# One list of pieces in place of four, in a chunked attention and cosine feed-forward kernel on one core

## The chip, the core and the metric

The kernel runs on one core of a Trainium2 chip. The metric is the time of one execution in microseconds of that core. TensorE (PE) does the matrix products, ScalarE (ACT), VectorE (DVE) and GpSimd (POOL) the elementwise work, and SyncE (SP) issues every DMA of the loops from one queue.

## The reference, cut to what matters

```python
def _attn_ref(q, k, v):                 # 8 batches, 8 heads, 576 tokens, head size 64, chunks of 64
    scores = scale * np.matmul(q_c, k_c.transpose(0, 1, 2, 4, 3))
    scores = scores - np.max(scores, axis=-1, keepdims=True)
    attn = np.exp(scores)
    attn = attn / (np.sum(attn, axis=-1, keepdims=True) + 1e-09)
    out = np.matmul(attn, v_c)
...
def _moe_ref(x, w_in, w_out):           # x 4608 x 512, w_in 512 x 2048, w_out 2048 x 512
    h = x @ w_in
    g = h * np.cos(h)
    return (g @ w_out).astype(np.float32)
```

Attention is done within chunks of 64 tokens. Its output, 4,608 rows of 512, goes through a feed-forward layer with the activation h·cos(h). All is float32.

## The kernel before, in words

The rows are cut into nine tiles of 512 tokens. The feed-forward layer runs over 16 blocks of 128 hidden units (`fc`, 0 to 15). Every float32 operand of a product is split into a high and a low part, and a product is the sum of three matrix products (high·high, high·low, low·high).

**Stage 1** takes tiles 1 and 0 in 32 steps `s` (L1207). Each step makes one block of h (`hidden`, 12 matmuls into one of two `h` banks), then h·cos(h) by a chain of six operations (`activated`, L690: ACT, DVE, ACT, DVE, a copy to the high part, a subtraction for the low part), and, three steps later (`LAG`), four out pieces (`project`, three matmuls each, one per block of 128 rows). The attention of tiles 0, 1 and 2 is woven in. The products of steps 29 to 31 are left for stage 2.

**Stage 2 and later** handle tiles in pairs with a scheme of seven products (A11, S3, S2, A12, A22, S1, S4) in place of eight. It wants the weights `w_in` as sums of blocks ("combos"). They are computed in stage 1 on DVE, ACT and POOL (L1285 to L1296, and `combined`, L1794), stored to DRAM (`keep_blocks`, `keep_sums`, 256 KB each, 56 of them) and streamed back, two combos at a time, into rooms of the `w_in` tiles (`load_two`, L854). A streamed load has seven rooms at first and four (`KEPT_ROOMS`) afterwards: when the second product of a room has been issued, the room is loaded again. In the first round (28 loads) a load is two DMAs of 256 KB, later one of 512 KB. Tile 2 is done by `two_pairs` (four rounds of seven products and 16 out pieces), tiles 3 and 4, 5 and 6, 7 and 8 by eight `wide_pair` and one `second_tile` each (units u = 1, 2, 3).

**The order** is written out by hand in tables. Each step is a *piece* (`piece`, L1007): an engine, an estimated length, a function that emits its instructions, the pieces that it comes after, and a `lag` after its end. The numbers of a piece (length, lag, predecessors) served the planner that made the tables; the kernel at hand reads only the tables: `in_order` (L258) sorts the pieces by their rank and emits them, and a second table names the pieces that go to their other engine. Every instruction is kept in the order of its engine's list (`tc.keep_in_program_order`), and waits on data are put in as needed. There are four lists: stage 1; tile 2 with unit 1; unit 2; unit 3 (742, 1,010, 596 and 463 pieces). `emit` (L1321) and `close` (L1354) put a list out, empty it and clear all links, so that a piece of one list names no piece of an earlier one:

```python
    def close(wanted, *when):
        emit(wanted, *when)
        stream[0] = last_high[0] = None
        for d in (spent, low_of, acc_free, readers, ...): d.clear()
```

Two sorts of transfers are no pieces before: the streamed loads of `product` (L938) come wherever the PE piece stands that frees the room, and the stores of finished output rows (`finish`, L761) are left free to be placed.

Of the kernel before, what the change touches and what calls it, by code (L numbers as in the profile page):

```python
# [90 lines left out]
RANK_FIRST = (  # L91
# [33 lines left out]
)  # L125

ELSEWHERE_FIRST = (
# [7 lines left out]
RANK_SECOND = (  # L135
# [53 lines left out]
)  # L189


RANK_NEXT = (
# [1756 lines left out]
```

## Time and profile before

| | us |
|---|---|
| median of 3 runs | 797.67 (797.0 to 797.83) |
| the profiled execution | 796.2 |
| its span, first to last instruction | 794.4 |
| PE busy in the span | 773.2 |
| mean granted PE clock | 0.993 |

The profile is of one execution. Its time is 1.8 us over its span (launch and end), and 1.5 us under the median. "PE busy" counts the time in which at least one matmul is in flight.

### The profile page before, as it was taken

The page shows a single profiled execution, that of the slowest core. Times are in us where ns is not written, and L with a number is a line of the kernel's source. Part 1 is how long each engine was busy: PE and PEld are TensorE (multiplying, and loading weights), DVE is VectorE, ACT ScalarE, POOL GpSimd, SP SyncE. Part 2 cuts the span into 40 slices and gives each one's busy share as a digit, 9 for nine tenths or more (in the row PEclk, how much of TensorE's full clock was granted, in tenths as well). Part 3 has the DMA queues.
Part 4 walks back from the last instruction along what each step waited for, and adds up shares of the span by engine and source line. Part 5 has one row for each costly group of instructions (what it writes and reads, how often), then busy time and mean ns, then how long its engine had stood idle before and what let it go on. Part 6 is the DMA issues. An engine that isn't in the chain of part 4 may idle for free.

```text
span 794.4 us, 15040 instructions
## 1 busy us (share of the span) xinstructions
PE 773.2 (97%) x5818; PEld 676.2 (85%) x5818; DVE 589.0 (74%) x1031; ACT 431.3 (54%) x782; POOL 177.5 (22%) x158
## 2 busy tenths in 40 slices
PE   7999999997799999999999999999999999999997
PEld 6888888885798898888888888888888888888886
DVE  6998878997588868877788788776796756465632
ACT  5998876463485555554564256445533555445220
POOL 1352038735234352010110131100110200001010
PEclk9999999999899999999999999999999999999999
DMA  9994305248899764774555656666365164555441
GB/s 337 406 418 179 107 1 173 100 167 290 288 330 293 245 227 134 239 238 146 186 158 199 211 176 214 221 215 224 122 194 178 41 205 153 173 171 160 159 127 59
DMA packets 75928, 156.19 MB, mean 197 GB/s; under 512 B 7632, under 2 KB 22224, under 8 KB 75856
## 3 DMA queue, kind: packets, MB, share of 16 engines
q1 hardware_dynamic: 75856, 155.22, 57.2%
q8 instruction: 46, 0.75, 0.4%
q14 instruction: 26, 0.21, 0.1%
HBM read 117.44 MB, written 37.75 MB: 195 GB/s over the span
## 4 chain that ended last, share of the span: by engine, by line
PE 87%; DMA 9%; SPq 1%; ACT 1%; DVE 1%; issue 0%; DVEq 0%; ACTq 0%
PE acc L299 45%; PE h L299 33%; PE a L299 10%; DMA w_in<-combo 3%; DMA combo<-w_in 2%; DMA vt<-in_v_dram 2%; SPq L296 1%; DMA x<-partial 1%; DMA qt<-in_qT_dram 1%; DVE pts L614 0%; ACT w L380 0%; PE a L588 0%; ACT x L659 0%; ACT half L382 0%; ACT L699 0%
## 5 line engine op out<-in xcount | busy, mean ns | idle before, releaser
L299 PE MATMUL acc<-w_out,g_hi 128*128 128x512 f32 x1124 | 336.1, 381 | 5.8 <-ACT g_hi L316 5.8
L299 PEld LDWEIGHTS acc<-w_out,g_hi 128*128 128x128 f32 x1124 | 209.5, 189 | 35.3 <-ACT g_hi L316 6.2
L299 PE MATMUL h<-x,w_in 128*128 128x512 f32 (+1 forms) x960 | 228.5, 367 | 4.4 <-DMA w_in<-combo 4.1
L299 PE MATMUL acc<-w_out,g_lo 128*128 128x512 f32 x562 | 212.9, 379 | 0.0
L299 PEld LDWEIGHTS h<-x,w_in 128*128 128x128 f32 x960 | 172.5, 192 | 26.9 <-issue 4.3
L320 POOL TENSOR_TENSOR g_lo<-g,g_hi 128x512 fp32r<-128x512 f32 x35 | 47.7, 1364 | 356.4 <-DVE g_hi L314 192.4
L299 PEld LDWEIGHTS acc<-w_out,g_lo 128*128 128x128 f32 x562 | 106.3, 189 | 15.4 <-POOL g_lo L320 0.2
L299 PE MATMUL h<-w_in,w_in 128*128 128x512 f32 (+1 forms) x384 | 97.9, 353 | 0.6 <-DMA w_in<-combo 0.6
L299 PEld LDWEIGHTS h<-w_in,w_in 128*128 128x128 f32 x384 | 66.2, 190 | 8.8 <-DMA w_in<-combo 0.8
L316 ACT CAST g_hi<-g 128x512 fp32r<-128x512 f32 x61 | 37.8, 619 | 53.5 <-PE acc L299 30.9
L320 DVE TENSOR_TENSOR g_lo<-g,g_hi 128x512 fp32r<-128x512 f32 x73 | 54.6, 752 | 16.2 <-ACT g_hi L316 14.5
L951 DVE SCALAR_TENSOR_TENSOR g<-g,h 128x512 f32<-128x512 int32 x28 | 19.2, 686 | 52.4 <-ACT g L948 52.1
L955 ACT ACTIVATE g<-g 128x512 f32<-128x512 f32 x56 | 35.2, 629 | 20.6 <-DVE g L951 20.4
L299 PE MATMUL a<-w_in,w_in 128*128 128x512 f32 (+1 forms) x192 | 41.2, 353 | 0.4 <-DMA w_in<-combo 0.4
L299 PE MATMUL a<-x,w_in 128*128 128x512 f32 (+1 forms) x192 | 41.2, 353 | 0.0
L942 ACT COPY h<-h 128x512 f32<-128x512 f32 x28 | 16.0, 570 | 40.3 <-PE h L299 34.1
L299 PEld LDWEIGHTS a<-w_in,w_in 128*128 128x128 f32 x192 | 33.2, 190 | 4.8 <-issue 0.8
L955 ACT ACTIVATE w_in<-w_in 128x512 f32<-128x512 f32 x48 | 29.9, 628 | 12.4 <-DVE w_in L951 12.1
L299 PEld LDWEIGHTS a<-x,w_in 128*128 128x128 f32 x192 | 33.1, 190 | 4.0
L942 ACT COPY a<-h 128x512 f32<-128x512 f32 x28 | 16.1, 574 | 36.5 <-PE h L299 36.3
L697 ACT ACTIVATE g<-h 128x512 int32<-128x512 f32 x32 | 19.0, 597 | 26.4 <-PE h L299 24.7
L698 DVE SCALAR_TENSOR_TENSOR g<-g,h 128x512 f32<-128x512 int32 x32 | 21.7, 681 | 9.9 <-ACT g L697 9.7
(219 smaller groups left out, 1161.6 us busy)
## 6 DMA issues: line engine op xcount, KB each, us to landing
w_in<-combo SPq DMA_DIRECT2D x84, 512.0 KB, 3.7
combo<-w_in SPq DMA_DIRECT2D x56, 256.0 KB, 3.3
w_in<-combo SPq DMA_DIRECT2D x56, 256.0 KB, 5.1
gathered<-w_in SPq DMA_DIRECT2D x48, 256.0 KB, 3.5
qt<-in_qT_dram SPq DMA_DIRECT2D x36, 256.0 KB, 5.2
kt<-in_kT_dram SPq DMA_DIRECT2D x36, 256.0 KB, 5.3
w_in<-in_w_in_dram SPq DMA_DIRECT2D x16, 512.0 KB, 9.6
w_out<-in_w_out_dram SPq DMA_DIRECT2D x16, 512.0 KB, 9.6
```

The source lines that it names most:

```text
L296: kept(nc.sync.dma_start(out=out, in_=in_))
L299: kept(nc.tensor.matmul(*args, **kw))
L316: kept(nc.scalar.copy(out=out, in_=in_))
L320: kept(eng.tensor_tensor(out, a, b, op=op))
L697: lambda: kept(nc.scalar.activation(n, h, AF.Identity, bias=0.25, scale=0.5 / math.pi)),
L698: lambda: kept(nc.vector.scalar_tensor_tensor(g, n, -2.0 * math.pi, h, op0=turns, op1=over)),
L942: kept(nc.scalar.copy(out=out, in_=in_))
L951: kept(nc.vector.scalar_tensor_tensor(g, g.bitcast(I32), -2.0 * math.pi, h, op0=ALU.mult, op1=ALU.add))
L955: kept(nc.scalar.activation(g, g, AF.Sin, bias=0.5 * math.pi))
```

## The change

All 2,949 pieces stand in one list with one table of ranks, put out once at the end. The links that `close` cut are made: the first pieces of stage 2 now name the pieces of stage 1 that they need. Each streamed load and each store of output rows is a piece on SP with a rank of its own, and the stores are kept in order. The `lag` of nearly all SP pieces, 2.5 to 5.0 before, is 2.0. No arithmetic, tile or transfer is added or taken away.

```diff
-def in_order(work, wanted, rank, elsewhere):
+def in_order(work, rank, elsewhere):
...
-        nc.sync.dma_start(out=to, in_=os)
+        made_rows[t, sub, half, whole] = (to, os)
+    def store_rows(t, sub, half=None, whole=True):
+        to, os = made_rows.pop((t, sub, half, whole))
+        kept(nc.sync.dma_start(out=to, in_=os))
...
-        if n % 2 and fc in KEPT_ROOMS:
-            load_two(fc)
...
-        kept_sums[k] = piece(SP, 2.6, lambda k=k: keep_sums(k), lows[-1], lag=3.5)
-        for fc in (2 * k, 2 * k + 1):
-            if STREAM <= fc < STREAM + ROOMS:
-                piece(SP, 1.3, lambda fc=fc: load_two(fc, fc - STREAM), kept_sums[k], kept_sums[1], kept_sums[0])
+        kept_sums[k] = piece(SP, 2.6, lambda k=k: keep_sums(k), lows[-1], lag=2.0)
+    stream_room = list(range(STREAM, STREAM + ROOMS))
+    def stream_in(i, *after):
+        fc, q = stream_room[i], i // 7
+        first = i < len(combos)
+        stored_pairs = [d[k] for d in (kept_blocks, kept_sums) for k in (2 * q, 2 * q + 1)] if first else []
+        stream_here[i] = piece(SP, 1.3, lambda: load_two(fc, i), *after, *stored_pairs, lag=2.0)
...
-    emit([(i, -4.0) for i in parts_x + [kept_sums[k] for k in range(3)] + [summed]], RANK_FIRST, ELSEWHERE_FIRST)
+    low_of.update({(0, NFC - LAG + i): given[STAGE - LAG + i] for i in range(LAG)})
+    readers.update({
+        "h1": [held[STAGE - 2]], "h0": [held[STAGE - 1]], "a0": [banks_free["a", 0]], "a1": [banks_free["a", 1]],
+        "h2": [kept_sums[1], kept_blocks[1]], "more": [hids[-1]], "differences": [hids[-1]],
+    })
...
     def product_piece(n, length, run, *after):
-        p = pe(length, run, *after, stored_sums.get(n))
+        p = pe(length, run, *after, stream_here[n // 2])
         if n % 2:
-            room_done[n // 2] = p
+            i = n // 2
+            room_done[i] = p
+            if stream_room[i] in KEPT_ROOMS and len(stream_room) < UNITS * len(combos):
+                stream_room.append(stream_room[i])
+                stream_in(len(stream_room) - 1, p)
...
-            close([], RANK_LAST, ELSEWHERE_LAST)
             break
...
+    for i, by in in_order(work, RANK, ELSEWHERE):
+        work[i][2](*([by] if work[i][8] else []))
```

The tables are long rows of ranks, and a piece's number is its place in the order of the calls of `piece`. Read off in that way, the orders around the seam between stage 1 and tile 2 are these (out s/b is the out piece of step s and row block b, fc 13 to 15 of tile 0 are the products of steps 29 to 31, st0 to st6 are streamed loads):

```
PE before: hidden 30, 4 outs of step 28, hidden 31 | out fc14, scores 3a, scores 3b, 9 outs of fc13-15,
           A11, S3, S2, A12, A22, S1, 2 outs, S4, scores 4a
PE after:  hidden 30, hidden 31, 3 outs of step 28, 1 of step 27, scores 3a, 1 out of step 28, out fc13, scores 3b,
           out fc13, A11 (half), 3 outs of fc13-15, A11 (half), 2 outs, S3, S2, A12, A22, S1, 3 outs, S4, 2 outs, scores 4a
SP before: ... sums 2, sums 3, sums 5, q and k of tile 3, blocks 7, st6, st1, st0, partial rows, blocks 6, sums 4,
           st4, st3, st5, st2 | q and k of tile 4, ...
SP after:  ... blocks 4, blocks 6, sums 1, blocks 3, blocks 5, sums 3, blocks 7, tile 1's rows, q and k of tile 3,
           sums 4, sums 2, sums 5, st5, st4, st1, st0, partial rows, st2, st6, v of tile 3, st3, q and k of tile 4, st7, ...
```

## Rows read from the trace of the kernel before

**Rows 1.** Busy time by stretch, whole span: us, busy by engine, PEclk, DMA share, GB/s.

```profile
0.00:20.00 20.00, 14.61 (x292) 12.30 (x292) 12.24 (x25) 11.84 (x34) 3.22 (x8) 1.00 0.92 337
20.00:190.00 170.00, 169.77 (x1260) 146.88 (x1252) 153.46 (x263) 126.89 (x210) 75.72 (x73) 1.00 0.52 196
190.00:200.00 10.00, 4.25 (x19) 2.79 (x22) 4.29 (x7) 3.07 (x6) 1.27 (x1) 0.82 1.05 381
...
280.00:780.00 500.00, 500.00 (x3288) 437.06 (x3287) 352.55 (x607) 239.77 (x400) 68.35 (x50) 1.00 0.54 177
780.00:795.00 15.00, 9.64 (x51) 8.27 (x49) 3.39 (x6) 1.26 (x3) 0.00 (x0) 0.96 0.19 71
```

**Rows 2.** Waits of PE, whole span: us in total, times, longest us.

```profile
PE acc L299 <- ACT g_hi L316: 5.8, 1, 5.8
PE h L299 <- DMA w_in<-combo: 4.7, 2, 4.1
```

**Rows 3.** Timeline of PE, 188 to 265 us: start, us, instruction, [idle before <- releaser].

```profile
189.81 2.75 PE L299 MATMUL h<-x,w_in 128*128 128x512 f32 x12
198.31 1.22 PE L299 MATMUL acc<-w_out,g_hi 128*128 128x512 f32 x2 [5.75 <-ACT g_hi L316]
...
216.27 4.54 PE L299 MATMUL h<-x,w_in 128*128 128x256 f32 x24 [4.12 <-DMA w_in<-combo]
...
226.06 0.27 PE L299 MATMUL h<-kt,qt 64*64 64x64 f32 x1
...
227.15 0.70 PE L299 MATMUL acc<-w_out,w_in 128*128 128x512 f32 x2
...
243.77 0.94 PE L299 MATMUL h<-w_in,w_in 128*128 128x256 f32 x6 [0.57 <-DMA w_in<-combo]
...
263.73 0.91 PE L299 MATMUL a<-w_in,w_in 128*128 128x256 f32 x6 [0.38 <-DMA w_in<-combo]
```

**Rows 4.** Busy time by stretch around the seam, columns as in rows 1.

```profile
196.30:203.20 6.90, 4.89 (x127) 4.10 (x131) 2.50 (x5) 1.07 (x3) 0.00 (x0) 0.51 1.04 370
205.00:214.00 9.00, 7.15 (x45) 6.42 (x43) 8.92 (x17) 7.05 (x35) 2.76 (x3) 1.00 0.59 168
216.80:220.20 3.40, 3.40 (x19) 3.40 (x18) 0.29 (x1) 1.11 (x2) 0.00 (x0) 0.50 1.07 390
```

**Rows 5.** Timeline of ACT after hidden 31.

```profile
192.66 1.09 ACT L697 ACTIVATE g<-h 128x512 int32<-128x512 f32 x2 [2.45 <-PE h L299]
```

**Rows 6.** The chain that ended last, 160 to 272 us: start, us, what.

```profile
162.04 1.09 PE a L299 x64
...
176.92 2.59 PE acc L299 x12
179.51 2.59 PE h L299 x12
...
269.88 1.34 PE h L299 x12
```

**Rows 7.** Timeline of the SP queue: DMA issues around the seam.

```profile
163.34 1.29 SPq L761 DMA_DIRECT2D out_dram<-pts  x2
...
189.93 4.16 SPq L296 DMA_DIRECT2D w_in<-combo  x6
...
...
207.59 3.66 SPq L296 DMA_DIRECT2D w_in<-combo  x8
```

**Rows 8.** Waits of the SP queue, 170 to 265 us.

```profile
SPq L296 <- DMA combo<-w_in: 7.8, 4, 5.9
```

**Rows 9.** DMA, 185 to 275 us: traffic, then issues, KB each, median us to landing.

```profile
DMA packets 17345, 27.44 MB, mean 305 GB/s; under 512 B 1680, under 2 KB 6327, under 8 KB 17335
...
w_in<-combo SPq DMA_DIRECT2D x50, 256.0 KB, 5.2
```

**Rows 10.** DMA issues, 300 to 780 us.

```profile
w_in<-combo SPq DMA_DIRECT2D x80, 512.0 KB, 3.7
```

**Rows 11.** Waits of the SP queue, whole span.

```profile
SPq L761 <- ACT half L316: 23.4, 4, 13.9
```

More of the change, by code (lines that the diff above doesn't have):

```diff
@@ L848, in w_in_room, with load_two @@
         return wts.tile([P, 2 * TOK + PAD], dtype, name=f"w_in{fc}")
-    asked = [ROOMS]
     UNITS = 1 + (NT - FAST) // 2
-    def load_two(fc, i=None):
-        if i is None:
-            i = asked[0]
-            asked[0] += 1
+    def load_two(fc, i):
         if i < UNITS * len(combos):
@@ L929, in product @@
     def product(n, out, x_hi, x_lo, begin=False):
-        w, fc = streamed[n // 2]
+        w, _ = streamed[n // 2]
         w = w[:, n % 2]
@@ L1051, in attention_then_cos_ffn @@
     turn_of = sorted(due, key=lambda b: (due[b], b))
+    u = None
     for i, (name, fc) in enumerate(turn_of):
@@ L1055, in attention_then_cos_ffn @@
         back = turn_of[i - 2] if i > 1 else None
-        u = piece(ACT, 0.52, rest_of(key, 0), split.get(back), at=here[name, fc])
+        u = piece(ACT, 0.52, rest_of(key, 0), split.get(back), u, at=here[name, fc])
         l = piece(ACT, 0.52, rest_of(key, 1), joined.get(back), at=here[name, fc])
@@ L1124, in values_next @@
                         load_v(t, j)
-                more_values = piece(SP, 1.3, values_next, now, lag=3.0)
+                more_values = piece(SP, 1.3, values_next, now, lag=2.0)
             for i in (0, 2):
@@ L1181, in values_next @@
                         load_v(t, hp)
-                third_here.append(piece(SP, 1.3, values_next, w, lag=3.0))
+                third_here.append(piece(SP, 1.3, values_next, w, lag=2.0))
             for i in range(2):
@@ L1189, in queries_next @@
                 load_qk(t + 1, hp)
-        piece(SP, 5.2, queries_next, w)
+        queries_at.append(piece(SP, 5.2, queries_next, w, lag=2.0))
         return w
@@ L1205, in attention_then_cos_ffn @@
     third = None
+    begun = None
     third_here = []
+    queries_at = []
     for s in range(STAGE):
@@ L1215, in attention_then_cos_ffn @@
                 stream = piece(
-                    PE, 0.648, go, stream if cc else None, split["in", fc], bank_at, *x_done[t][2 * cc : 2 * cc + 2],
+                    PE, 0.648, go, stream if cc else begun, split["in", fc], bank_at, *x_done[t][2 * cc : 2 * cc + 2],
                     *(all_turned if s < 2 else ()), pairs=3, main=True,
                 )
+                begun = begun if cc else stream
             before.append(stream)
@@ L1229, in prefetch_third @@
                     load_qk(2, hp)
-            third_here.append(piece(SP, 5.2, prefetch_third, ahead[HP - 1], stream, lag=3.0))
+            third_here.append(piece(SP, 5.2, prefetch_third, ahead[HP - 1], stream, lag=2.0))
         if s >= LAG:
@@ L1248, in attention_then_cos_ffn @@
                     out_of[run_of[u] + 1, sub] = done
-                    stored.append(piece(SP, 0.65, lambda: None, done, lag=2.5))
+                    stored.append(piece(SP, 0.65, lambda tu=tu, sub=sub, fu=fu: store_rows(tu, sub, None, fu == NFC - 1), done, lag=2.0))
                     if u < GROUP:
-                        partial_out.append(done)
+                        partial_out.append(stored[-1])
                 if u < GROUP:
@@ L1256, in values_third @@
                             load_v(2, hp)
-                    third_here.append(piece(SP, 1.3, values_third, *partial_out, lag=3.0))
+                    third_here.append(piece(SP, 1.3, values_third, *partial_out, lag=2.0))
         key = ("g", s)
@@ L1273, in attention_then_cos_ffn @@
             third = attend_third(hid)
-    piece(SP, 2.6, resume, hid)
+    resumed = piece(SP, 2.6, resume, hid, lag=2.0)
     kept_blocks = {}
@@ L1282, in attention_then_cos_ffn @@
         kept_blocks[k] = piece(
-            SP, 2.0, lambda k=k: keep_blocks(k), split["in", 2 * k], split["in", 2 * k + 1], hids[GROUP + 6 + k], lag=3.5
+            SP, 2.0, lambda k=k: keep_blocks(k), split["in", 2 * k], split["in", 2 * k + 1], hids[GROUP + 6 + k], lag=2.0
         )
@@ L1296, in attention_then_cos_ffn @@
         lows.append(piece(DVE, 1.7, lambda by, k=k: low_parts(k, by), a, port=True, other=(POOL, 3.6, False)))
-        kept_sums[k] = piece(SP, 2.6, lambda k=k: keep_sums(k), lows[-1], lag=3.5)
-        for fc in (2 * k, 2 * k + 1):
-            if STREAM <= fc < STREAM + ROOMS:
-                piece(SP, 1.3, lambda fc=fc: load_two(fc, fc - STREAM), kept_sums[k], kept_sums[1], kept_sums[0])
+        kept_sums[k] = piece(SP, 2.6, lambda k=k: keep_sums(k), lows[-1], lag=2.0)
+    stream_room = list(range(STREAM, STREAM + ROOMS))
+    stream_here = {}
+    def stream_in(i, *after):
[3 more added lines that the diff above has]
+        stream_here[i] = piece(SP, 1.3, lambda: load_two(fc, i), *after, *stored_pairs, lag=2.0)
+    for i, fc in enumerate(stream_room):
+        stream_in(i, kept_sums[fc // 2], kept_blocks[fc // 2])
     def of_x(i, *args):
@@ L1319, in attention_then_cos_ffn @@
         parts_x.append(piece(DVE, 0.69, of_x(2, j), a, port=True))
-    def emit(wanted, *when):
-        for i, by in in_order(work, wanted, *when):
-            work[i][2](*([by] if work[i][8] else []))
-        work.clear()
-    emit([(i, -4.0) for i in parts_x + [kept_sums[k] for k in range(3)] + [summed]], RANK_FIRST, ELSEWHERE_FIRST)
     queue = deque((0, fc, sub) for fc in range(NFC - LAG, NFC) for sub in range(NSUB))
@@ L1348, in attention_then_cos_ffn @@
     g_pool = deque([(0, NFC - 3), (0, NFC - 2), (0, NFC - 1)])
-    g_extra = deque([None])
-    g_free = deque([None, None])
     queries_read = deque()
     keys_read = [()] * HP
-    def close(wanted, *when):
-        emit(wanted, *when)
-        stream[0] = last_high[0] = None
-        for d in (
-            spent, low_of, acc_free, readers, room_done, stored_sums, kept_g, queries_here, values_here, weighed,
-            taken, turned_all, x_lows, asked_out,
-        ):
-            d.clear()
-        for q, nothing in ((g_free, None), (queries_read, ()), (keys_read, ())):
-            for i in range(len(q)):
-                q[i] = nothing
+    low_of.update({(0, NFC - LAG + i): given[STAGE - LAG + i] for i in range(LAG)})
[3 more added lines that the diff above has]
+    })
+    g_free = deque(given[STAGE - 2 + i] for i in range(2))
+    spent["room"] = [kept_sums[2], kept_blocks[2]]
+    g_extra = deque(["room"])
+    for g in range(2):
+        queries_here[FAST + 1, g] = queries_at[0]
+    weighed[FAST] = parts_x
+    for i, j in enumerate((A11, S3, S2, A12, A22, S1, S4)):
+        x_lows[FAST, j] = [parts_x[i]]
     def pe(length, run, *after):
@@ L1380, in out_piece @@
             PE, 0.648 if half is None else 0.336, lambda: out_part(t, fc, sub, half), low_of.get(made_of(t, fc, sub)),
-            acc_free.get(sub), main=True,
+            acc_free.get(sub), *(by_run[2, sub] if t == 0 else ()), main=True,
         )
@@ L1388, in out_piece @@
             if len(made[half]) == 2:
-                piece(ACT, 0.4, lambda: finish(t, sub, acc[sub], True, ACT, half), *made[None], *made[half])
+                p = piece(ACT, 0.4, lambda: finish(t, sub, acc[sub], True, ACT, half), *made[None], *made[half])
+                piece(SP, 0.35, lambda: store_rows(t, sub, half), p, lag=2.0)
         elif not to_come[t, sub, half]:
             if t == 0:
-                acc_free[sub] = piece(DVE, 0.7, lambda: finish(t, sub, acc[sub], True, None), *made[None])
+                acc_free[sub] = piece(DVE, 0.7, lambda: finish(t, sub, acc[sub], True, None), *made[None], resumed)
             else:
                 acc_free[sub] = piece(
-                    ACT, 0.62, lambda by: finish(t, sub, acc[sub], True, by), *made[None], other=(DVE, 0.69, False)
+                    ACT, 0.62, lambda by: finish(t, sub, acc[sub], True, by), *made[None],
+                    *(rows_stored[t - 1] if t > FAST else [kept_sums[7]]), other=(DVE, 0.69, False),
                 )
+            rows_stored.setdefault(t, []).append(piece(SP, 0.65, lambda: store_rows(t, sub), acc_free[sub], lag=2.0))
     to_come = {}
+    rows_stored = {}
     def outs(n=None):
@@ L1453, in go @@
                     product(
-                        14 * q + 2 * j + i, v[out][:, i * HALF : (i + 1) * HALF], halves_x[j][:, 0], halves_x[j][:, 1],
+                        14 * q + 2 * j + i, v[out][:, i * HALF : (i + 1) * HALF], x_halves[FAST][j][:, 0], x_halves[FAST][j][:, 1],
                         bool(begin) and not i,
                     )
-                done[j] = product_piece(14 * q + 2 * j + i, 0.672, go, *(() if i else deps))
+                x = x_lows[FAST, j] if q == 0 else ()
+                done[j] = product_piece(14 * q + 2 * j + i, 0.672, go, *(() if i else (*deps, *x)))
             return done[j]
@@ L1590, in keep @@
                 kept(nc.sync.dma_start(out=gathered[fc], in_=v[g]))
-            kept_g[fc] = piece(SP, 0.65, keep, m, lag=4.0)
+            kept_g[fc] = piece(SP, 0.65, keep, m, lag=2.0)
         readers["kept"] = [kept_g[2 * k], kept_g[2 * k + 1]]
@@ L1616, in second_tile @@
                     free = [g_free.popleft(), g_free.popleft()]
-                here = piece(SP, 1.3, begin, kept_g[fc], kept_g[fc + 1], *free, lag=4.2)
+                here = piece(SP, 1.3, begin, kept_g[fc], kept_g[fc + 1], *free, lag=2.0)
             lows[fc] = parts_of_g(t, fc, lambda fc=fc: v[fc], here)
@@ L1640, in queries_for @@
             free = [i for hp in (2 * g, 2 * g + 1) for i in (*queries_read.popleft(), *keys_read[hp])]
-            queries_here[t, g] = piece(SP, 2.6, go, *free, lag=5.0)
+            queries_here[t, g] = piece(SP, 2.6, go, *free, lag=2.0)
     def values_for(t, *after):
@@ L1647, in go @@
                     load_v(t, hp)
-            free = () if t == FAST + 1 else x_taken()
+            free = x_taken()
             if g:
                 free = [room_done[T_LOAD]] if t == FAST + 1 else [*free, *queries_read.popleft(), *queries_read.popleft()]
-            values_here[t, g] = piece(SP, 1.3, go, *after, *free, lag=4.5)
+            values_here[t, g] = piece(SP, 1.3, go, *after, *free, lag=2.0)
     def scores_now(t):
@@ L1809, in parts @@
             return lows
-        l6 = parts(6)
-        k6 = piece(SP, 2.6, lambda: keep_sums(6), *l6, lag=4.0)
+        l6 = parts(6, summed, kept_blocks[6])
+        k6 = kept_sums[6] = piece(SP, 2.6, lambda: keep_sums(6), *l6, lag=2.0)
         w7 = piece(DVE, 1.38, lambda by: whole_again(7, by), *l6, port=True, other=(POOL, 2.5, False))
         s7 = piece(DVE, 1.7, lambda by: sums_of_w(7, by), w7, port=True, other=(POOL, 3.0, False))
-        k7 = piece(SP, 2.6, lambda: keep_sums(7), *parts(7, s7), k6, lag=4.0)
-        rooms = list(range(STREAM, STREAM + ROOMS))
-        for n in range(1, 7 * NPAIR, 2):
-            if rooms[n // 2] in KEPT_ROOMS:
-                last = 2 * (len(rooms) // 7) + 1
-                stored_sums[n] = k7 if last >= 7 else k6 if last >= 6 else None
-                rooms.append(rooms[n // 2])
+        k7 = kept_sums[7] = piece(SP, 2.6, lambda: keep_sums(7), *parts(7, s7, kept_blocks[7]), k6, lag=2.0)
         stored_sums["six"] = k6
@@ L1835, in attention_then_cos_ffn @@
             if n_pair == 0:
-                first_copies = list(acc_free.values())
+                first_copies = list(rows_stored[0])
             n_pair += 1
@@ L1889, in attention_then_cos_ffn @@
             outs()
-            close([], RANK_LAST, ELSEWHERE_LAST)
             break
-        ends = wide_x(t, lambda j, part: [used])
-        ends += [(low_of[t - 1, NFC - 2], 0.0), (low_of[t - 1, NFC - 1], 0.0)]
-        close(ends, *((RANK_SECOND, ELSEWHERE_SECOND) if u == 1 else (RANK_NEXT, ELSEWHERE_NEXT)))
+        wide_x(t, lambda j, part: [used])
+    for i, by in in_order(work, RANK, ELSEWHERE):
+        work[i][2](*([by] if work[i][8] else []))
 _OUTS = [((4608, 512), "float32")]
```

22 lines of the change are left out of this document (3 added, 19 removed), and 300 rows, old and new, of tables (ELSEWHERE, ELSEWHERE_FIRST, ELSEWHERE_SECOND, RANK).

## The prediction

> **What bounds the kernel now.** I read first the busy time by stretch [rows 1]. From 20 to 190 us PE is busy for 169.77 of 170 us and from 280 to 780 us for 500 of 500, at the full clock: there the time is matmul work, and the change adds and removes none. The first 20 us have 5.4 us without a matmul and the end has 5.4 us (15 less 9.64, some 0.6 of it past the span). What is left lies between 190 and 280 us, around the seam between the first and the second list. Then the waits of PE [rows 2] name two: 5.8 us for a high part of g, 4.1 us for a streamed load. The timeline [rows 3] puts them: hidden 31 begins at 189.81 and ends at 192.56; the next matmul is an out piece at 198.31, after 5.75 us; then 4.12 us before 216.27, and 0.57 and 0.38 us later. Sum 10.82 us.
>
> The stretches around them [rows 4] show a second cost. From 196.3 to 203.2 and from 216.8 to 220.2 us the granted clock is half, 1.2 GHz in place of 2.4, each time just after PE had stood still. PE was busy for 4.89 and 3.40 us in them; at half speed half of that is lost, 4.1 us. So the seam costs 10.8 + 4.1 = 14.9 us.
>
> **Why PE stands there.** The first wait: the last pieces of list one put g's first step of steps 30 and 31 together at 192.66 [rows 5], after hidden 31, and the second list, which knows nothing of g, begins with an out piece of step 30. So PE has nothing in hand for the length of a chain of six operations. The second wait is SP's: it issued three streamed loads at 189.93 and the next ones only at 207.59 [rows 7], having waited up to 5.9 us for a store of combos to land [rows 8]. In the meantime, 205 to 214 us, the DMA engines were 0.59 busy [rows 4], while they were full from 190 to 200 [rows 1] and at 217 [rows 4].
>
> **The change, part by part.** *Order at the seam.* After hidden 31 PE now gets four outs of steps 27 and 28, scores 3a, an out, an out of fc13, scores 3b, an out of fc13 and half of A11 before an out of fc14, and one more out before fc15. Durations: an out 0.65 (four in 2.59), a hidden 2.59, two products of six matmuls 1.34 [rows 6], one group of scores 1.09 (226.06 to 227.15) [rows 3]. That is 4 x 0.65 + 1.09 + 0.65 + 0.65 + 1.09 + 0.65 + 0.67 = 7.4 us before fc14, and 8.1 before fc15. The chain needed 5.75 us, and g of step 30 now starts ahead of hidden 31's end. The four outs used to run before hidden 31, so this adds no work; hidden 31 merely comes 3.2 us (five outs) sooner, near 186.6. The 5.75 us go. Cover: if those outs and scores were themselves late (scores need the two h banks, freed by the chains of steps 30 and 31), at worst the same 5.75 us come back. DVE, which carries the chains, was busy for only 4.29 of the 10 us after 190 [rows 1], so there is room.
>
> *Loads at the seam.* SP's order is new: combos 6 and 7 (blocks) and sums 4 go ahead of the partial rows, and st5, st4, st1, st0 are issued right behind sums 5. The data before them: tile 1's rows (1 MB, at 163.34 as now [rows 7], right after the weighted products of tile 2 at 162.04 [rows 6]), q and k of tile 3 (2 MB), sums 4, 2 and 5 (3 MB). At the 381 GB/s of the full queue [rows 1] 6 MB take 15.7 us, to 179, and landed near 182. The four loads (2 MB) take 5.5 us and land near 190. A11 is wanted at 186.6 + 2.6 + 6.7 = 195.9, so it has 6 us in hand. The partial rows wait for hidden 31 (189.2), then 1 MB, st2, st6, v of tile 3 and st3 (3 MB, 7.9 us) are in near 200 with 3 us for the landing; S2 and A12, their first users, come at 195.9 + 0.67 + 1.94 + 0.67 + 1.30 + 1.34 = 201.8 and after. The 4.12 us go too. Bounds: 0, if the sum above holds, to 4.12, the wait now; as the margins are 2 to 6 us I take 0.7, near the lower end.
>
> *Later loads of the first round.* Their room is freed by a product, and the PE work between that and the use, counted from the tables with the durations above, is the cover. Before, the shortest are 4.7 us (loads 12 and 26); after, 4.7 (load 18) and 5.3 (12, 19). A load of this stretch lands 5.2 us after its issue [rows 9], and the wait of 0.57 us at 243.77 [rows 3] is load 12, as 5.2 less 4.7 says. The wait of 0.38 us is load 18, which SP issued behind sums 7; now it stands ahead of them. So I take 0.5 us for load 18 and bound it by 0 and 3 (all three late, DMA fuller). The Trainium skill, DMA: Bandwidth & Descriptors, section "Anatomy of one DMA", gives a DMA (of GpSimd's path) a fixed 2.0 us plus its bytes at 436 GB/s, which is also the lag that the new pieces carry. By it 256 KB land in 2.6 us (an estimate from that page), load 18 is not late, and the sum would be 0.5 us lower; the row's 5.2 speaks against it here.
>
> *Links, ranks and stores elsewhere.* In the wide units a load lands in 3.7 us [rows 10] and the new tables leave at least 5.3 us of PE work behind its place. Inside the old lists PE waited for 0.23 us in 20 to 190 and for nothing in 280 to 780 [rows 1]; I take 0.2 us for the whole new list, bounds 0 to 3. The 33 stores of rows are issued as before, now at fixed places. The first 14 PE pieces and the loads ahead of the lists are in the same order: 0, bounds -0.5 to +0.5. At the end the last two copies go to two engines instead of one, the last store is issued as late: 0, bounds -0.3 to +0.3.
>
> *Clock.* With no wait over 1 us at the seam the 4.1 us come back; that hangs on the two waits above.
>
> **Sum.** 14.9 - 0.7 - 0.5 - 0.2 = 13.5 us. The profiled execution of 796.2 us (span 794.4, 1.8 around it) becomes 782.7; the median shown is 1.5 above it, so 797.67 becomes **784.2 us**.
>
> **Rivals.** *The DMA takes over as the bound.* For: from 190 on the queue is full, and 185 to 275 us moved 27.44 MB at 305 GB/s [rows 9]; PE cannot run 15 us ahead of data that arrive no sooner. Then the gain is what the queue itself wins: its idle share in 205 to 214, 0.41 x 9 = 3.7 us [rows 4], and the 1.75 MB (blocks 6, sums 4) stored ahead of the first loads, 4.6 us at 381 GB/s. Together 8.3: 789.4 us. Against: all of stage 1 up to 190 used the engines by half only [rows 1], and the new order fills that.
>
> *The wait is moved, not removed.* PE finds another operand late at the seam (scores behind the h banks, x behind DVE), and its clock falls again: one wait of 5.75 us and half of 4.1 stay, 7.8 less gain, 792 us. Should all of it return, there is no change. Against: more than 7 us of ready work stand in the table.
>
> *Slower: the fixed SP order holds loads back in the wide units.* SP has waited for up to 13.9 us with one store of rows for a copy [rows 11], while such stores were free to be placed; now rows, gathered g and streamed loads stand in one fixed order. (The Trainium skill, DMA: Bandwidth & Descriptors, same section, says that a DMA's semaphore wait happens on the issuing sequencer, before dispatch; by that rule what stands behind it in the queue waits as well, and the row agrees that SP stood.) If each of the 24 wide pairs got one load 0.8 us late, 19 us go: 803 us. It decides from 0.65 us a pair on (15.1 in all). Against: the shortest cover of 5.3 us is 1.6 above the landing time.
>
> **How the numbers follow.** Forecast 0.67 (782.8, with nothing late, to 787); DMA bound 0.16; moved wait 0.07 with a gain, 0.03 without; slower 0.07. Range 782.5 to 791: it holds the first two and their bounds. A measurement here can tell about 0.2%, 1.6 us, from no change. Faster 0.67 + 0.16 + 0.07 = 0.90, same 0.03, slower 0.07.
>
> **What would show it.** Right: PE's busy time is some 769 us (773.2 less 4.1), the granted clock stays full from 20 us to the end, no PE wait over 1 us after 20 us, the first A11 comes 12 to 14 us sooner, SP issues st0 before hidden 31 begins. Wrong: a PE wait on w_in<-combo of several us between 190 and 260 us (DMA bound), on g_hi or g (moved wait), or many waits of under 1 us after 280 (slower).

## The result, and the profile after

The changed kernel takes 784.36 us (median of 4 runs, 783.78 to 785.35); the kernel before, on the same chip, 797.51 us (4 runs, 797.0 to 797.83). The ratio is 0.9837, interval 0.982 to 0.9854. The profiled execution of the changed kernel took 784.27 us, its span 782.5.

Busy time by stretch of the changed kernel, columns as in [rows 1]:

```profile
0.00:20.00 20.00, 14.79 (x292) 13.00 (x292) 11.27 (x22) 10.90 (x32) 5.55 (x11) 0.91 0.91 336
20.00:190.00 170.00, 169.09 (x1262) 146.63 (x1252) 156.17 (x274) 127.38 (x211) 73.93 (x70) 1.00 0.59 217
190.00:200.00 10.00, 10.00 (x170) 8.53 (x169) 9.19 (x17) 7.31 (x26) 3.96 (x5) 1.00 0.96 339
200.00:210.00 10.00, 9.30 (x73) 8.84 (x72) 6.92 (x14) 7.44 (x25) 4.28 (x5) 1.00 1.05 387
210.00:220.00 10.00, 10.00 (x173) 8.64 (x172) 8.91 (x18) 7.61 (x16) 4.48 (x3) 1.00 0.79 288
...
240.00:280.00 40.00, 39.51 (x407) 36.58 (x398) 31.60 (x58) 23.29 (x42) 13.62 (x11) 1.00 0.73 241
...
sum 780.00, PE 769.79 PEld 673.64 DVE 577.54 ACT 435.54 POOL 186.33; mean PE 96.22 PEld 84.21 DVE 72.19 ACT 54.44 POOL 23.29
```

From 190 to 200 us PE had been busy for 4.25 us at a clock of 0.82 [rows 1]; now it is busy for all 10 at the full clock, and DVE for 9.19 in place of 4.29. The half-clock stretches of [rows 4] are gone. What is left at the seam is 0.70 us and 0.49 us. The waits of PE say for what:

```profile
PE acc L304 <- DMA kt<-in_kT_dram: 1.9, 1, 1.9
PE h L593 <- POOL e L325: 1.7, 3, 1.0
...
PE h L304 <- DMA w_in<-combo: 1.2, 2, 0.7
```

The wait for g_hi of [rows 2] is gone; the 4.7 us for w_in<-combo are 1.2. The two larger waits lie in the first 20 us. Timeline of PE (as [rows 3]) and of the SP queue (as [rows 7]) at the seam of the changed kernel:

```profile
184.45 5.34 PE L304 MATMUL h<-x,w_in 128*128 128x512 f32 x24
...
196.74 0.83 PE L304 MATMUL h<-x,w_in 128*128 128x256 f32 x6
...
204.86 1.62 PE L304 MATMUL h<-x,w_in 128*128 128x256 f32 x12 [0.70 <-DMA w_in<-combo]
```

```profile
187.22 3.67 SPq L301 DMA_DIRECT2D w_in<-combo  x8
190.99 3.07 SPq L301 DMA_DIRECT2D x<-partial  x4
194.80 3.19 SPq L301 DMA_DIRECT2D w_in<-combo  x4
198.10 1.23 SPq L301 DMA_DIRECT2D vt<-in_v_dram  x2
199.46 0.96 SPq L301 DMA_DIRECT2D w_in<-combo  x2
```

Hidden 30 and 31 are the 24 matmuls from 184.45, so 31 begins near 187.0 and ends at 189.6. A11, the first line with 128x256 tiles, begins at 196.74. Before, it began at 209.31, so it comes 12.6 us sooner; PE's timeline of the kernel before:

```profile
209.31 1.50 PE L299 MATMUL h<-x,w_in 128*128 128x256 f32 x12
```

SP issues four loads (two DMAs of 256 KB each) ahead of the partial rows, where it had issued three and then waited until 207.59 [rows 7].

To place the difference, one cut serves for all kernels of this study: the hidden that waits for g just behind 28 us in every trace. From its start to the end of the last matmul each has the same 5406 matmuls. The busy time of that stretch, first in the kernel before, then in the changed one:

```profile
28.62:789.64 761.02, 750.19 (x5406) 657.02 (x5406) 566.98 (x987) 411.09 (x735) 173.50 (x150) 0.99 0.56 191
```

```profile
29.19:777.10 747.91, 746.72 (x5406) 653.60 (x5406) 556.54 (x972) 415.22 (x747) 177.48 (x154) 1.00 0.57 194
```

This middle part became 13.11 us shorter: PE's idle time in it fell from 10.83 to 1.19 us, and its busy time, for the same matmuls, from 750.19 to 746.72, which is the half clock. The start lost 0.57 us (29.19 less 28.62); the end, from the last matmul to the end of the span, grew from 4.76 to 5.40. Sum: 11.90 us, the difference of the spans.

### The profile page after: what moved, and what is told of

Its sections match the earlier page's. It is cut to its first block, busy times and chain, and to the rows that moved or that the text cites. A ratio compares the mean times of both kernels' runs of the same rounds, so it can differ in the third digit from the quotient of the medians.

```text
span 782.5 us, 15047 instructions
## 1 busy us (share of the span) xinstructions
PE 769.8 (98%) x5818; PEld 673.6 (86%) x5818; DVE 577.5 (74%) x1012; ACT 435.5 (56%) x793; POOL 186.3 (24%) x166
## 4 chain that ended last, share of the span: by engine, by line
PE 93%; DMA 4%; ACT 1%; DVE 1%; SPq 0%; issue 0%; POOL 0%; DVEq 0%; POOLq 0%
PE acc L304 47%; PE h L304 35%; PE a L304 11%; DMA w_in<-combo 2%; DMA x<-partial 1%; DMA kt<-in_kT_dram 1%; SPq L301 0%; POOL e L325 0%; PE a L593 0%; ACT w L385 0%; DVE m L482 0%; ACT x L664 0%; DVE x L667 0%; DVE g L705 0%; DVE x L319 0%
## 5 line engine op out<-in xcount | busy, mean ns | idle before, releaser
L304 PE MATMUL acc<-w_out,g_hi 128*128 128x512 f32 (+1 forms) x1124 | 335.6, 380 | 0.0
L304 PE MATMUL acc<-w_out,g_lo 128*128 128x512 f32 (+1 forms) x562 | 212.6, 378 | 0.0
L325 POOL TENSOR_TENSOR g_lo<-g,g_hi 128x512 fp32r<-128x512 f32 x44 | 60.5, 1376 | 263.7 <-ACT g_hi L321 127.6
L325 DVE TENSOR_TENSOR g_lo<-g,g_hi 128x512 fp32r<-128x512 f32 x64 | 45.5, 713 | 23.4 <-ACT g_hi L321 21.8
L955 DVE SCALAR_TENSOR_TENSOR g<-g,h 128x512 f32<-128x512 int32 x28 | 19.2, 685 | 49.0 <-ACT g L952 49.0
L959 ACT ACTIVATE g<-g 128x512 f32<-128x512 f32 x56 | 35.1, 626 | 12.7 <-DVE g L955 12.6
L325 POOL TENSOR_TENSOR g_lo<-w_in,g_hi 128x512 fp32r<-128x512 f32 x11 | 14.2, 1293 | 109.9 <-ACT g_hi L321 70.5
L702 ACT ACTIVATE g<-h 128x512 int32<-128x512 f32 x32 | 19.0, 595 | 21.4 <-PE h L304 20.6
L952 ACT ACTIVATE g<-h 128x512 int32<-128x512 f32 x28 | 16.7, 598 | 25.0 <-PE h L304 23.8
```

Source lines behind the costliest of these rows:

```text
L304: kept(nc.tensor.matmul(*args, **kw))
L325: kept(eng.tensor_tensor(out, a, b, op=op))
L702: lambda: kept(nc.scalar.activation(n, h, AF.Identity, bias=0.25, scale=0.5 / math.pi)),
L952: kept(nc.scalar.activation(g.bitcast(I32), h, AF.Identity, bias=0.25, scale=0.5 / math.pi))
L955: kept(nc.vector.scalar_tensor_tensor(g, g.bitcast(I32), -2.0 * math.pi, h, op0=ALU.mult, op1=ALU.add))
L959: kept(nc.scalar.activation(g, g, AF.Sin, bias=0.5 * math.pi))
```

## The experiments

The theory: all of the gain is made at the seam, by the orders of the queues there; the one list, its links and the pieces for loads and stores bring nothing by themselves. The rivals: either wait can be had alone; or the gain is spread over the new order of later units; or the places of loads and stores are what counts.

The edits use one helper: `moved(rank, (a, b, c))` puts pieces b and c right behind piece a and leaves the rest in order.

**1. PE's order alone, in the four old lists.**

```diff
+RANK_FIRST = moved(RANK_FIRST, (653, 659),
+    (665, 668, 669, 667, 666, 660, 661, 662, 670, 671, 663, 672, 673, 674, 664, 675))
+RANK_SECOND = moved(RANK_SECOND, (36, 21), (37, 20, 23, 22, 24))
```

> The kernel before, with only the order of PE, ACT and DVE around the seam taken from the changed kernel: at the end of list one hidden 31 goes ahead of four outs of steps 27 and 28, and the second list begins with scores and outs of fc13 ahead of the outs of fc14. The order on SP is the old one. Theory (the two waits at the seam come from two orders and one can't be had without the other): the wait of 5.75 us for g_hi goes, but A11 and A12 then ask sooner for streamed loads that SP issues behind the partial rows and the stores of sums, and those come forward only as far as hidden 31 does, 2.6 to 3.2 us. So the wait for w_in<-combo grows from 4.1 to 8 to 10 us, the clock still falls once, and the time is 793 to 795 us against 797.5. Rival (the costs add): 5.75 us and 2.4 us of half clock go and the second wait stays at 4.1 us: 789.4 us.

Measured: 796.88 us (10 runs), ratio 1.0005 (0.9985 to 1.0025). No change that these runs can tell, so the rival's 789.4 fell, and the theory gave too much: the wait for a load that it saw growing to 8 to 10 us stayed at 3.60. PE's timeline:

```profile
190.15 4.41 PE L318 MATMUL h<-x,w_in 128*128 128x512 f32 x12 [2.26 <-DVE g L719]
...
208.52 2.90 PE L318 MATMUL h<-x,w_in 128*128 128x256 f32 x12 [2.19 <-issue]
...
216.58 5.46 PE L318 MATMUL h<-x,w_in 128*128 128x256 f32 x24 [3.60 <-DMA w_in<-combo]
```

The 5.75 us for g_hi are gone, and 2.26 + 2.19 us stand in their place, with the wait for a load at 216 nearly as it was. The middle part is 762.86 us, 752.88 of them busy: the clock fell three times (0.50 from 192 to 194, again behind 208 and behind 216). The profiled execution is one of the slower ones (798.64 us). The first wait, ahead of hidden 31, was new to me. For the second, ahead of A11, the profile names no cause (`issue`). A DVE operation of scores 3 that reads an h tile ended at 208.42, 0.07 us before A11's first weights were loaded, so A11 may have waited for that bank; no run tests it.

**2. SP's order alone.**

```diff
+RANK_FIRST = moved(RANK_FIRST, (536, 683), (711, 684, 491, 712, 699),
+    (719, 720, 714, 706, 700), (676, 707, 721, 713))
```

> The kernel before, with only SP's order at the seam taken from the changed kernel: combos 6 and 7 and sums 4 are stored ahead of the partial rows, and four streamed loads are issued right behind sums 5. The order of PE is the old one. Theory: the wait of 5.75 us for g_hi and the half clock after it (2.4 us) stay; the waits for w_in<-combo (4.1, 0.6 and 0.4 us) and the half clock after 216.8 us (1.7 us) go: 790 to 792 us. Rival 1 (SP's order brings nothing by itself, since PE's order is what matters): 797.5 us. Rival 2 (the DMA engines are the bound, so that the loads land no sooner): over 794 us, with a wait for w_in<-combo of over 2 us left.

Measured: 791.07 us (7 runs), ratio 0.9927 (0.9905 to 0.9949), as the theory said. The wait for g_hi stands unchanged, and a load is late once, by 1.2 us:

```profile
PE acc L317 <- ACT g_hi L334: 5.8, 1, 5.8
...
PE h L317 <- DMA w_in<-combo: 1.2, 1, 1.2
```

The middle part is 755.53 us, 5.5 less than before.

**3. Both orders, in the four old lists.** Edits 1 and 2 together.

> The kernel before, with both orders at the seam, PE's and SP's, in the four old lists: no links across the stages, rows stored and later loads issued as before. Theory: that is the whole gain; the one list, its links, the kept stores of rows and the order of later units are worth nothing: 783 to 785.5 us, no wait of PE over 1 us from 20 us on, full clock. If the start of the changed kernel lost time, this kernel is up to 1.5 us faster than the changed one. Rival (a part of the gain is in the order of the first round after the seam or in the units): 788 us or more, with waits for w_in<-combo after 220 us. Second rival (the changed kernel's links or stores cost time that its seam pays for): under 782.5 us.

Measured: 787.47 us (4 runs), ratio 0.9881 (0.9846 to 0.9915): between theory and rival. One wait of 2.27 us is left where run 1 had it, and the clock is at 0.83 from 190 to 200. The timeline of DVE has its cause (L340 with half and w are the sums of pair 6, L720 is the last link of step 29's chain):

```profile
185.81 1.17 DVE L930 TENSOR_TENSOR x<-vt,x 128x512 fp32r<-128x512 f32 x1
186.91 1.82 DVE L340 TENSOR_TENSOR half<-w 128x256 f32<-128x256 f32 x2
188.65 0.41 DVE L340 TENSOR_TENSOR half<-half,w 128x256 f32<-128x256 f32 x1
189.09 0.42 DVE L340 TENSOR_TENSOR half<-w,half 128x256 f32<-128x256 f32 x1
189.44 0.68 DVE L720 TENSOR_TENSOR g<-h,g 128x512 f32<-128x512 f32 x1
```

Hidden 31 needs the h bank that this last link frees. Moved four outs ahead, it comes before DVE is done with the sums that stand in front. So there is a third order in the change, DVE's.

**4. Three orders.** Run 3, and the sums of pair 6 on POOL with the whole form on DVE, and the low part of g of step 28 on DVE, as the change has them:

```diff
+ELSEWHERE_FIRST = tuple(sorted({*ELSEWHERE_FIRST, 723} - {642, 722}))
```

> The four old lists with both orders at the seam, PE's and SP's, and a third thing of the change: the sums of pair 6 are made on POOL instead of DVE (its whole form on DVE instead of POOL), and the low part of g of step 28 on DVE. Without it PE lost 2.27 us ahead of hidden 31, which waited for the last link of step 29's chain, 189.44 on DVE, behind 3.4 us of sums; the clock was at 0.83 from 190 to 200. Theory (the gain at the seam hangs on three queues, PE, SP and DVE, and any one left as it was keeps a wait): that wait and the half clock go, no PE wait over 1.2 us after 20 us, full clock from 20 us on: 4 to 5 us faster than with two orders, 0.981 to 0.985 of the kernel before. Rival 1 (the late g is due to something else, so that the wait stays): the same as with two orders, 0.988. Rival 2 (POOL, slower at sums, makes the low part of step 29 late, so that PE waits at the outs of fc13): in between, with a wait on g_lo.

Measured: 783.58 us (4 runs), ratio 0.9833 (0.981 to 0.9855), the changed kernel's own ratio. The wait ahead of hidden 31 is 0.49 us, DVE ends the link at 187.3, and POOL has the sums beside it (timelines of PE, DVE and POOL):

```profile
187.34 2.86 PE L320 MATMUL h<-x,w_in 128*128 128x512 f32 x12 [0.49 <-DVE g L721]
```

```profile
186.61 0.68 DVE L721 TENSOR_TENSOR g<-h,g 128x512 f32<-128x512 f32 x1
```

```profile
183.89 2.25 POOL L341 TENSOR_TENSOR half<-w 128x256 f32<-128x256 f32 x2 [1.90 <-DVE w L341]
```

Its middle part is 748.90 us, 746.65 of them busy, against 747.91 and 746.72: no half clock, and 1 us more of small waits. So the four old lists, with three orders changed at the seam, reach the time of the one list. Which part is due to the sums and which to the low part of g, no run separates.

**5. The changed kernel with SP's old order at the seam.** The other way round:

```diff
+RANK = moved(RANK, (650, 723, 718, 717), (676, 709, 721, 720, 722, 719))
```

> The changed kernel with SP's order at the seam as before, all other queues as changed: loads 6, 1 and 0 ahead of the partial rows, then the partial rows, sums 4, and only then loads 4, 3, 5 and 2 (blocks 6 stay early, the one list asks for it). Theory (SP's order is a part of the gain that the others need): A12 and the products after it wait for streamed loads, 4 to 8 us on w_in<-combo between 200 and 225 us, and the clock falls once: 5 to 10 us slower than the changed kernel, 0.990 to 0.996 of the kernel before. Rival (with the DMA engines full either way, the loads land no sooner in the new order): within 2 us of the changed kernel.

Measured: 791.92 us (5 runs), ratio 0.9935 (0.9913 to 0.9956), as the theory said. Waits of PE, then busy time by stretch:

```profile
PE h L319 <- DMA w_in<-combo: 6.9, 2, 5.8
```

```profile
200.00:210.00 10.00, 4.18 (x26) 3.94 (x25) 3.69 (x8) 2.78 (x17) 4.24 (x5) 0.84 0.93 314
210.00:220.00 10.00, 10.00 (x64) 9.71 (x64) 5.40 (x11) 5.95 (x10) 1.04 (x1) 0.82 1.03 349
```

The middle part is 756.27 us. Put together, by the middle part of one profiled execution each, which leaves start and end out (the whole runs of the kernel before scattered from 793.9 to 800.3 us beside runs 1 to 3):

| kernel | middle, us | PE idle in it | PE busy in it |
|---|---|---|---|
| before | 761.02 | 10.8 | 750.2 |
| PE's order alone | 762.86 | 10.0 | 752.9 |
| SP's order alone | 755.53 | 6.9 | 748.6 |
| PE's and SP's | 753.35 | 4.8 | 748.6 |
| PE's, SP's and DVE's | 748.90 | 2.3 | 746.7 |
| changed, SP's order old | 756.27 | 6.9 | 749.4 |
| changed | 747.91 | 1.2 | 746.7 |

The parts don't add. In these executions PE's order gains nothing by itself (it is 1.8 us longer, but the ten runs show no change), 2.2 us beside SP's, and 6.6 with DVE's too; SP's gains 5.5 by itself and 8.4 in the changed kernel. How far the middle part scatters is known for the changed kernel alone.

**6. Loads and rows issued as before, in the one list.** First both; then, on another chip, the rows alone beside the unaltered changed kernel.

```diff
-        made_rows[t, sub, half, whole] = (to, os)
+        nc.sync.dma_start(out=to, in_=os)
...
-        stream_here[i] = piece(SP, 1.3, lambda: load_two(fc, i), *after, *stored_pairs, lag=2.0)
+        now = (lambda: load_two(fc, i)) if i < ROOMS else (lambda: None)
+        stream_here[i] = piece(SP, 1.3, now, *after, *stored_pairs, lag=2.0)
```

(The freed room's load is then issued at the end of the product.)

> The changed kernel, but the streamed loads after the first four rooms are issued with the product that frees the room, and the rows of the output are stored with the copy that makes them, as in the kernel before; the one list and all its ranks stay. Theory: neutral, 783.5 to 785.5 us, since the place of a load or store on SP behind the seam has cover either way (the shortest is 5.3 us against a landing of 3.7 to 4.5 us). Rival (the fixed places of loads and stores on SP are what keeps the loads in time): 787 us or more, with many waits for w_in<-combo in the wide units, each under 1 us. Second rival (the fixed places hold loads back): 782.5 us or less.

> The changed kernel, unaltered, beside the three that differ from it by one thing each, on the same chip: 784.4 us, or as much of the kernel before as in the comparison shown (0.984). It is the base line for the other three. No theory differs on it.

> The changed kernel, but each store of output rows is issued with the copy that makes the rows, as before; the streamed loads stay pieces. The run with loads and stores both as before lost 1.60 and 0.64 us on PE between 216 and 220 us, waiting for k of tile 4, with row stores on SP ahead of them. Theory (the stores of rows are what was in the way: at their copy they stand ahead of the loads of q and k): the same waits, 1.5 to 3 us slower than the changed kernel. Rival 1 (the loads' places are what counted): within 0.7 us of the changed kernel, no wait for k. Rival 2 (the chip's state that day): neither.

Measured: both as before, 787.87 us (4 runs, 786.3 to 790.95), ratio 0.9897 (0.9851 to 0.9942); rows alone 784.97 us, ratio 0.9852 (0.9837 to 0.9868); unaltered 783.96 us, ratio 0.9837 (0.9821 to 0.9853). Of both as before, PE and SP:

```profile
218.31 0.24 PE L304 MATMUL h<-kt,qt 64*64 64x64 f32 x1 [1.60 <-DMA kt<-in_kT_dram]
219.65 0.24 PE L304 MATMUL h<-kt,qt 64*64 64x64 f32 x1 [0.64 <-DMA kt<-in_kT_dram]
```

```profile
206.87 2.00 SPq L301 DMA_DIRECT2D w_in<-combo  x4
209.16 2.96 SPq L801 DMA_DIRECT2D combo<-w_in  x4
...
212.91 0.64 SPq L301 DMA_DIRECT2D kt<-in_kT_dram  x1
```

A k issued at 212.91 is waited for at 218.3. With the rows alone at their copies SP had two DMAs of loads there in place of four, issued that k at 211.08, and PE did not wait for it. So "neutral" was wrong: with the rows at their copies, the fixed places of loads are worth some 2 us in this one place. That is from one execution, and the interval of the ratio still touches the unaltered kernel's. The profiled execution took 786.7 us; what the two runs of 789 and 791 us lost besides isn't known. Loads alone as before were not run. The rows alone, 0.0015 above it with intervals that overlap, can't be told from no change: their middle part is 0.7 us longer (748.62) and their end 0.6 shorter.

**7. The end, the start and load 3.** Three small edits against what the profile of the changed kernel left: the order of the last copies and stores; load 3 behind load 2; two quotients of the first softmax back on DVE.

```diff
+RANK = moved(RANK, (2920, 2943, 2944, 2935, 2936, 2931, 2932))   # end
+RANK = moved(RANK, (719, 720))                                   # load 3
+ELSEWHERE = tuple(i for i in ELSEWHERE if i not in (182, 184))   # start
```

> The changed kernel with another order of the last six pieces alone: the rows of sub 2, whose last out piece is the fourth from the end, are copied and stored first, then sub 1, then sub 0. In the changed kernel DVE copied sub 1 first, at 776.49, so that sub 2 was copied a microsecond after it was complete and three stores were issued after 777.1. Theory (the end lost about a microsecond by this order): the last store is issued at once after the copy of sub 0, 778.4 in place of 779.6: 0.8 to 1.4 us faster than the changed kernel. Rival (the time from the last matmul to the end is the landing of the last store and its fixed end, whatever the order): within 0.3 us.

> The kernel with the new tail, and two edits more: streamed load 3 goes on SP directly behind load 2, ahead of v of tile 3, and two quotients of the first softmax, which the change had put on POOL, go back to DVE. Theory: the wait of 0.70 us for w_in<-combo near 204 us goes, since the load is issued 1.4 us sooner, and the waits for POOL's e in the first 25 us (1.7 us in three) shrink by 0.5 to 1.0 us: 0.7 to 1.7 us faster than the kernel with the new tail alone, some 782 us. Rival (v lands later and PE waits for it instead; DVE has no room at the start): no gain, or 0.5 us slower.

Measured beside the unaltered 783.96 us: the end alone 781.98 us (5 runs, 781.43 to 782.66), ratio 0.9814 (0.9798 to 0.9829); all three 783.78 us, ratio 0.9834 (0.9817 to 0.985). The end does what was expected: from the last matmul to the end of the span it takes 4.15 us (5.38 unaltered), and the middle part is the same (747.79). That is 1.2 us; the medians' other 0.8 is not accounted for. All three together are 1.8 us slower than the end alone, which two more runs took apart:

> The changed kernel with the new tail and streamed load 3 directly behind load 2, without the edit at the start. In the run with all three edits the wait of 0.7 to 1.2 us near 204 us was gone (PE busy for 10.00 of the 10 us from 200), but the first 30 us took 2.1 us longer than with the new tail alone (the same hidden began at 30.49 and at 28.36). Theory (the load is worth its wait, the start's edit ate it): 0.5 to 1.2 us faster than the new tail alone, 0.9795 to 0.981 of the kernel before, some 781 us. Rival (the load ahead of v is paid back later in the first round, or the start varies from run to run by itself): 0.981 to 0.9835, the same as the new tail alone or slower.

> The changed kernel with the new tail and the two quotients of the first softmax back on DVE, without the edit of load 3. Theory (DVE, busy for 9.73 of the 10 us from 10 with the edit, has no room for them, so that PE waits for z and later for pts, and its clock falls at the start): slower than the kernel with new tail and load 3 by 1.5 to 3.0 us, the first hidden behind 26 us begins near 30.3, clock under 0.9 somewhere in 10 to 25 us. Rival (the slow start was that one execution's, since loads at the start land at other times in each): it begins between 28 and 29 us, and the time is that of the new tail alone, 0.981 to 0.982 of the kernel before.

Measured: end and load 3, 781.87 us, ratio 0.9812 (0.9787 to 0.9837); end and start, 783.32 us, ratio 0.9833 (0.981 to 0.9857). Load 3 brings nothing. Busy time by stretch of that run:

```profile
200.00:210.00 10.00, 10.00 (x81) 9.68 (x80) 7.69 (x17) 7.94 (x26) 4.29 (x5) 1.00 1.03 375
...
240.00:280.00 40.00, 39.27 (x382) 36.35 (x381) 31.57 (x56) 22.73 (x41) 12.68 (x10) 1.00 0.75 256
```

The wait at 204 is gone, but a wait of 0.73 us, for an x from ACT, stands between 240 and 280, so that the middle part is 747.87 us. The start's edit makes PE wait for DVE's z (0.8 us) where it had waited for POOL's e; the hidden of the cut then begins at 28.87 here and at 30.49 with all three, so the larger part of that 30.49 was that execution's own. The hidden thus begins where the rival had it, but the time is above the rival's 0.982. Whether the edit costs anything beside that scatter isn't settled. The version with the end's order alone, 781.98 us, is 2.0 us faster than the changed kernel beside it.

## Why the prediction was right

The mechanism held: the waits at the seam went, and the full clock came back with them. The time (784.36 against 784.2) is nearer than the steps deserve. Against the profiled execution the sum gave 782.7, and 784.27 was measured, 1.6 us above it: 0.6 from the half clock, 0.6 each from start and end, less 0.2 that the waits gained. The 1.5 us that I added to get from the profiled execution to the median didn't carry over, since the changed kernel's profiled execution lay at its median. The two errors cancel; that is luck.

- **Waits at the seam.** Idle time in the middle part fell by 9.64 us. The sum had 10.8 less 1.4, that is 9.4. The total held, the places less so. A12 waited for 0.70 us where 0.7 had been taken near the lower end of a range up to 4.12, not worked out. Load 18, for which 0.5 was put, was in time: its product, A22 of the third round, begins at 247.72 without a wait. The 0.49 us stand at A11 of the fourth round, which reads load 21, where the sum had only its 0.2 for all the rest:

```profile
247.72 1.50 PE L304 MATMUL a<-w_in,w_in 128*128 128x256 f32 x12
...
263.04 0.91 PE L304 MATMUL h<-x,w_in 128*128 128x256 f32 x6 [0.49 <-DMA w_in<-combo]
```

  The unaltered kernel's execution in part 6 waited for 1.21 us at A12 and nowhere behind it. So the sum of some 1.2 us repeats, and that two terms came out to the tenth is luck.
- **Half clock.** 3.5 us came back, not 4.1. The step that halves the busy time of two stretches was over-sized by 0.6 us. It holds for the products: the 24 matmuls from 216.27 to 220.65 took 4.38 us, 3.40 of them at half clock, and 24 at the full clock take 2.68 (206.32 to 209.00 in the changed kernel), so they lost 1.70, the half of 3.40. It doesn't hold for the scores, most of the first stretch: two groups took 3.49 us (199.89 to 203.38), 3.3 of them at half clock, and 1.10 and 1.09 us at the full clock (192.31 to 193.41, 194.90 to 195.99). These 64x64 matmuls lost 1.3 us where half of 3.3 is 1.7; that is some 0.4 of the 0.6. First and next instruction of the two groups in the kernel before, then of one group in the changed one:

```profile
199.89 0.37 PE L299 MATMUL h<-kt,qt 64*64 64x64 f32 x1
...
203.38 0.70 PE L299 MATMUL acc<-w_out,g_hi 128*128 128x512 f32 x2
```

```profile
192.31 0.27 PE L304 MATMUL h<-kt,qt 64*64 64x64 f32 x1
...
193.41 0.70 PE L304 MATMUL acc<-w_out,g_hi 128*128 128x512 f32 x2
```

- **Order at the seam.** Hidden 31 was put at 186.6 and began near 187.0; A11 at 195.9 and began at 196.74; 0.57 us of either is the later start. I said that DVE had room because it was busy for 4.29 us of the 10 after 190. That was the wrong stretch: the room was wanted ahead of hidden 31, where DVE was full (run 3's rows have no gap from 185.81 to 190.1), and there the change makes it by giving the sums to POOL. The trace of the kernel before shows it as well: the link that frees the bank ended there at 189.50, behind the sums, and hidden 31 was wanted at 186.6:

```profile
188.82 0.68 DVE L700 TENSOR_TENSOR g<-h,g 128x512 f32<-128x512 f32 x1
```

  I had not costed that edit; runs 3 and 4 put it, with the low part of g, at 4.5 us of the middle part.
- **Loads at the seam.** I had the data ahead of the four loads landed near 182, and the loads landing near 190. SP issued them only from 187.22: the data ahead of them began 2 us later (165.33) and moved at 315 GB/s (165 to 187 us) in place of 381. The sign that I had named, st0 before hidden 31 begins, failed: st0, the last of the four, was issued at 189.97, and hidden 31 began near 187.0. SP had stood for 3.9 us until a store of sums 5 had landed (waits of the SP queue, 160 to 265 us):

```profile
SPq L301 <- DMA combo<-w_in: 5.1, 5, 3.9
```

  I had put 3 us for a landing; st0's two DMAs took 6.2 and 6.4 us and were in at 196.1 and 196.8. A11's halves, which read one each, begin at 196.74 and 199.35, so of the cover of 6 us 0.6 was left. The Trainium skill, DMA: Bandwidth & Descriptors, section "Anatomy of one DMA", says that a semaphore wait happens on the issuing sequencer, before dispatch. By that rule the loads behind the sums wait as well, and the trace agrees: no load was issued in these 3.9 us.
- **Start and end.** The start was put at 0 ± 0.5 and lost 0.57 us in this pair, but the same program's other execution began its hidden at 27.83, 0.8 sooner than before: no effect of the change is shown. The end was put at 0 ± 0.3 and lost 0.64. "The last store is issued as late" failed, as DVE copied sub 1 ahead of sub 2, which had been complete first, and three stores were left behind the last matmul; run 7 gives it back by order alone.
- **The other signs** held: PE's busy time is 769.79 us, the clock stays full behind 20 us, no wait of PE there is over 1 us in this execution (1.21 in the other), A11 comes 12.6 us sooner.
- **Rivals.** Of the DMA as the bound: from 200 to 210 the engines are at 1.05 and PE waits for 0.70 us, so it is near; but from 185.5 to 187.5 us they were only 0.24 busy, with SP standing until 187.22, so it is not the bound. The moved wait came in run 3, 2.27 us and a stretch of half clock, and the change escapes it by its third order. The fixed SP order in the wide units cost nothing:

```profile
280.00:770.00 490.00, 490.00 (x3208) 427.24 (x3208) 333.03 (x574) 236.64 (x399) 70.38 (x54) 1.00 0.53 177
```

## What to carry to other kernels

A stall at the border of two hand-ordered lists is a matter of all queues that meet there: moving PE's work forward alone brought nothing here, because other queues (DVE's sums, SP's loads) then ended last. Read the room of the helping engine in the stretch to which the work is moved, not in the one in which it stood. And to judge small terms, cut the span at two instructions that both kernels share: start, middle and end then scatter apart, and the changed kernel's middle repeats within 0.1 us (747.91 and 747.89) where its span varies by 1.4.

## What the runs showed of the hardware

The same program starts differently from one execution to the next. PE's timeline, then its busy time from 8 to 10 us, of the execution shown first:

```profile
7.31 4.56 PE L304 MATMUL acc<-kt,qt 64*64 64x64 f32 x96 [1.92 <-DMA kt<-in_kT_dram]
```

```profile
8.00:10.00 2.00, 2.00 (x44) 2.00 (x41) 0.94 (x2) 2.00 (x16) 0.00 (x0) 0.50 1.04 403
```

The same of the unaltered kernel's execution in part 6, whose span is 1.4 us shorter:

```profile
6.59 1.15 PE L304 MATMUL acc<-kt,qt 64*64 64x64 f32 x32 [1.24 <-DMA kt<-in_kT_dram]
```

```profile
8.00:10.00 2.00, 1.87 (x60) 1.76 (x61) 1.93 (x4) 2.00 (x16) 0.00 (x0) 1.00 1.00 375
```

The first k landed later in one, PE stood for 1.92 us and then ran at half clock; in the other it stood for 1.24 us and kept the full clock.

Under a full queue a transfer of 256 KB lands long after its issue, whichever tile it is for (DMA issues of the second execution, 195 to 225 us):

```profile
w_in<-combo SPq DMA_DIRECT2D x16, 256.0 KB, 5.2
...
combo<-w_in SPq DMA_DIRECT2D x4, 256.0 KB, 5.2
```

The time isn't fixed: of the eight DMAs from 187.22 on in the first execution, the first, issued into a nearly empty queue, landed after 3.1 us and the eighth after 6.4. An estimate from the second execution: at the 375 GB/s of 200 to 210 us, 5.2 us are 1.95 MB, seven to eight transfers in flight. So here the landing time of a transfer hangs on what was issued ahead of it, and the order of issue decides who is late.

At half clock not all matmuls lose the half: of 3.40 us at half clock the 24 matmuls of 128x256 lost 1.70, of some 3.3 us the 64x64 scores lost 1.3.
